# Attention in twelve batches of 2 to 4 chunks for fourteen of 3, with squares on VectorE, other opening matmuls and the last copy on ScalarE

## The chip, the core and the metric

The program runs on one core of one Trainium2 chip. The core has TensorE (PE in the rows, with PEld for its weight loads), VectorE (DVE), ScalarE (ACT), GpSimd (POOL) and SyncE (SP), which issues most of the transfers. Each engine takes its own instructions in program order and waits for the others through semaphores. The metric is the time of one execution on the device in microseconds (us).

## The reference

Sigmoid attention over 2 batches, 12 heads, 448 positions and 64 dimensions, then two MLPs on the 896 tokens of width 768. All in float32.

```python
def _attn_ref(q, k, v):                 # (2, 12, 448, 64) each
    scale = 1.0 / np.sqrt(q.shape[-1])
    scores = scale * np.matmul(q, k.transpose(0, 1, 3, 2)) - np.log(S)
    attn = 1.0 / (1.0 + np.exp(-scores))
    return np.matmul(attn, v)

def _moe_ref(x, w_gate, w_val, w_out, rms_g):     # 768 -> 1536 -> 768
    rms = np.sqrt(np.mean(x * x, axis=-1, keepdims=True) + 1e-06)
    xn = x / rms * rms_g
    g = xn @ w_gate
    return (g * (1.0 / (1.0 + np.exp(-g))) * (xn @ w_val) @ w_out)

def _moe2_ref(x, w_in, w_out):                    # 768 -> 2048 -> 768
    h = x @ w_in
    return (h * (1.0 / (1.0 + np.exp(-h))) @ w_out)
```

## The kernel before

**Attention.** Two heads are worked on together, as a pair: there are twelve pairs, six to a batch of the input. The 448 keys of a pair are cut into three chunks of 128 (c = 0 to 2) and a tail of 64 keys; the tails of two neighbouring pairs make one chunk together (c = 3, called with the even pair). That gives 42 chunks. `scores(i, c)` makes the scores of one chunk of pair i: three passes of matmuls, each for two heads (high times high, low times high, high times low parts of keys and queries), or one float32 pass for a tail and for the first chunk of pairs 0 and 1. They go into a tile of the pool `scp`, which has three, each two banks wide; then ScalarE applies the sigmoid (L387) and writes a tile of the pool `at`. `attend(i, c)` multiplies such a tile by the values (L405) into the accumulator of the pair, one bank of the pool `avp`, which has two. When a pair has its four contributions, `collect(i)` copies the accumulator to `xr` (VectorE, L420 or L425) and squares it (ScalarE, L423), and `add_square` adds the square to the batch's sum (VectorE, L431). `prep(i)` splits keys and queries of a pair into high and low parts (VectorE).

**Turns.** The loop at L530 runs over batches of `BATCH` = 3 chunks. In each turn it collects what is ready, issues the scores of the turn's batch (tail last), adds the squares, and then issues the attends of the batch before (tail first). Behind that come the letters of the turn's entry in `PLAN`: each `w` is the next step of `prologue`, each `n` the next step of `norm_first`. Nothing reorders these instructions (`manual_schedule`): the program's order is each engine's order.

`prologue` has 26 steps. They prepare six slabs of weights and cut the first four of them into high and low parts: for a slab s there is the exponent (ScalarE, L253), the shift (VectorE, L257), the merge (VectorE, L265) together with the load of the slab two ahead on SyncE's queue, the cast of two halves (ScalarE, L241) and their lower parts (VectorE, L244). In the order of the steps the cast of slab s-1 stands behind the exponent of slab s, and its lower parts behind the shift of slab s.

`norm_first` normalises the first batch of the input. Its steps: square sums (`square_sums`, eight one-column matmuls, L436); the first half of `rsqrt` (six small VectorE operations); the second half (six more, then `diag`, L456, 448 wide); an empty step; the spread of `diag` over all partitions (a matmul, L473) with ScalarE's copy `r` of it (L499); then eight steps of `normed`, in each of which one block of `xr` is scaled (L481), the one before it gets its high part (ScalarE, L241) and the one before that its low part (VectorE, L244).

**After attention.** The two MLPs follow. All their work is made of jobs for which `Plan.run` sets the order by costs and due times. It begins with a product of the normalised first batch (`g`, L730); behind that product the square sums of the second batch (L436) stand in TensorE's queue, one product later their spread (L473). The last block of the output is made in `mixed` (L831 on): the accumulator `e2x` is copied to `e2s` and sent out by SyncE.

**Opening.** While the first loads are under way TensorE runs `IDLE` = 8 matmuls on a tile of zeros (L515), into the tile `idle` of the pool `scp`.

Of the kernel before, what the change touches and what calls it, by code (L numbers as in the profile page):

```python
# [9 lines left out]
F32 = mybir.dt.float32  # L10
F32R = mybir.dt.float32r
BF16 = mybir.dt.bfloat16
U32 = mybir.dt.uint32
I32 = mybir.dt.int32
AF = mybir.ActivationFunctionType
ALU = mybir.AluOpType
PSUM = bass.MemoryType.PSUM

B, H, S, D = 2, 12, 448, 64
# [3 lines left out]
P = 128  # L23
CP = 112
NC = S // CP
KC = S // P
# [3 lines left out]
HALF = 3 * P  # L30
NT = B * S
EPS = 1e-6
BATCH = 3
DIRECT = ((0, 0), (1, 0))
IDLE = 8
SQUARED = 10
LAG = {"A": 0.105, "D": 0.081, "P": 0.165, "S": 4.4}
HOP = 0.4
# [5 lines left out]
ZI = True  # L44
ZE = False
LOADED = (6, 7)
PLAN = ",,ww,w,www,www,ww,ww,wwn,wwnn,wwnn,wwwnn,wwnn,wwnn,nn".split(",")
LOADS = (0, 2)
RING = 9
RESERVE = 6  # L50
# [143 lines left out]
def tile_attention_two_mlps(  # L194
# [9 lines left out]
    nc = tc.nc  # L204
# [8 lines left out]
    sp = ctx.enter_context(tc.tile_pool(name="sp", bufs=1))  # L213
# [103 lines left out]
    xr = [rp.tile([P, 2, 2, S], F32, tag=f"r{t}", name=f"xr{t}") for t in range(3)]  # L317
    ctx.enter_context(tc.manual_schedule())
    with ExitStack() as actx:
        ap = actx.enter_context(tc.tile_pool(name="ap", bufs=2))  # L320
        at = actx.enter_context(tc.tile_pool(name="at", bufs=8))
        pctx = ExitStack()
        psum = [pctx.enter_context(tc.tile_pool(name="scp", bufs=3, space=PSUM))]
        avp = pctx.enter_context(tc.tile_pool(name="avp", bufs=2, space=PSUM))
# [2 lines left out]
        kq, vr, ks, att, av, acc, sqs = {}, {}, {}, {}, {}, {}, {}  # L327
# [4 lines left out]
        def load_pair(i):  # L332
            b, hp = pairs[i]
            if i not in kq:
                pair_tile(i)
            if i:
                nc.sync.dma_start(kq[i], kqd[b, hp])
            else:
                for j, queue in enumerate((nc.sync, nc.scalar)):
                    queue.dma_start(kq[i][:, j], kqd[b, hp, :, j])  # L340
# [49 lines left out]
        begun = {}  # L390
# [24 lines left out]
        def collect(i):  # L415

            b, hp = pairs[i]
            ps = av.pop(i)[:, :S]
            if i < SQUARED:
                nc.vector.tensor_copy(xr[hp // 2][:, b, hp % 2], ps)  # L420
            which, home_ = ("s1", sqs) if hp else ("s0", acc)
            sq = home_[i if hp else b] = sp.tile([P, S], F32, tag=which, name=f"{which}{i}")
            nc.scalar.activation(sq, ps, AF.Square)  # L423
            if i >= SQUARED:
                nc.vector.tensor_copy(xr[hp // 2][:, b, hp % 2], ps)  # L425

        def add_square(i):

            b, hp = pairs[i]
            if hp:  # L430
                nc.vector.tensor_tensor(acc[b], acc[b], sqs.pop(i), ALU.add)  # L431
# [71 lines left out]
        n = len(pairs)  # L503
        normal = norm_first()
        load_pair(0)
        zeros = sp.tile([P, S], F32, tag="s3", name="zeros").bitcast(BF16)[:, :P]
        nc.vector.memset(zeros, 0.0)
        nc.vector.memset(warm, 0.0)
        nc.vector.memset(logs, -6.104793232414985)
        nc.vector.memset(ones, 1.0)  # L510
        nc.scalar.activation(warm, warm, AF.Sigmoid)
        row = zeros[:, None, :D].to_broadcast([P, S // D, D])
        idle = ps_tile("idle")
        for j in range(IDLE):
            nc.tensor.matmul(idle[:, j % 2, :S], zeros, row, start=True, stop=True)  # L515
        load_pair(1)
        pair_tile(2)
        nc.vector.memset(kq[2], 0.0)
# [7 lines left out]
        turn_, ready = 0, []  # L526
        chunks = []
        for i in range(0, n, 2):
            chunks += [(i, c) for c in range(KC + 1)] + [(i + 1, c) for c in range(KC)]
        batches = [chunks[j : j + BATCH] for j in range(0, len(chunks), BATCH)]  # L530
        for before, batch in zip([[]] + batches, batches + [[]]):
            for i in ready:
                collect(i)
            for i, c in sorted(batch, key=lambda u: u[1] == KC):
                if c == 0:
                    if i + 1 < n:
                        prep(i + 1)
                    if i + 3 < n:
                        load_pair(i + 3)
                        load_v(i + 3)  # L540
                    if i in LOADS:
                        load_next()
                scores(i, c)
            while ready:
                add_square(ready.pop(0))
            for i, c in sorted(before, key=lambda u: u[1] != KC):
                ready += attend(i, c)
            for what in PLAN[turn_]:
                if what == "w":
                    step()  # L550
                else:
                    next(normal, None)
            turn_ += 1
        collect(ready[0])
        add_square(ready.pop())


        for _ in normal:
# [15 lines left out]
    def dve(n, fn, deps=(), **more):  # L574
        return plan.add("D", 0.071 + n / 960, fn, deps, **more)
# [224 lines left out]
    sdone = [None] * 4  # L800
# [52 lines left out]
    def mixed(  # L853
        name, macs, slabs, keys, book, fdep, put, dest=None, home=None, ahead=True, own=None, finish=None, per=6
    ):


        n = len(keys)
        w = [6 * (slabs + i // per) + i % per for i in range(2 * n)]
        saved = {}  # L860

        def save(j, src, dep):
            def go():
                saved[j] = saved_tile(name, j)
                nc.scalar.activation(saved[j], src(), AF.Copy)

            return scalar(S, go, [dep, sdone[j]], psum=True)

        def add(j, src, deps, m=None, b=None):
            def go():  # L870
                d = saved[j] if m is None or dest is None else dest(m, b)
                tt(d, src(), saved[j], ALU.add)

            a = dve(S, go, deps, need=home.ready if dest and m is not None else None)
            if m is not None:
                sdone[j] = put(m, b, lambda: saved[j] if dest is None else dest(m, b), a) or a
            return a

        g = lambda ps, a, **k: group(macs, ps, a, book, fdep, own, **k)
        if ahead:  # L880
            bx, by = Banks(f"{name}x"), Banks(f"{name}y")
            ba, bb = Banks(f"{name}a", True), Banks(f"{name}b", True)
            bz, bv, bu, bw = ba.bank(0), ba.bank(1), bb.bank(0), bb.bank(1)
            done = []
            for k in range(0, n, 2):
                for m, t in enumerate((ba, bb)):
                    i = 2 * k + 2 * m
                    done += product(
                        [t.bank(0), t.bank(1)], w[i : i + 2], keys[k : k + 2], (0, 1), first=k == 0,
                        final=k == n - 2 and m > 0, take="ps" if k == 0 else None, start=t.start if k == 0 else None,  # L890
                    )
            u = save(3, bu, done[-1])
        else:
            bx, by, bz, bw = (Banks(f"{name}{c}") for c in "xyzw")
        g1 = g(bx, "A11", start=True, first=bx)
        v0 = save(0, bx, g1)
        g2_ = g(by, "S1", start=True, first=by)
        v1 = save(1, by, g2_)
        g3 = g(bx, "S2", deps=[v0])
        v2 = save(2, bx, g3)  # L900
        g4 = g(bz, "A12", start=not ahead, stop=ahead, first=None if ahead else bz)
        if ahead:
            a00 = add(0, bz, [g4, v0], 0, 0)
        g5 = g(bx, "S3", deps=[v2])
        a11 = add(1, bx, [g5, v1])
        if ahead:
            c11 = add(1, bw, [a11], 1, 1)
            bb.read_by(u, c11)
        g6 = g(by, "S4", stop=ahead, deps=[v1])
        if ahead:  # L910
            a01 = add(2, by, [g6, v2])
            c01 = add(2, bv, [a01], 0, 1)
            by.read_by(v1, a01)
            ba.read_by(a00, c01)
        g7 = g(bx, "A22", stop=ahead, deps=[a11])
        if ahead:
            a10 = add(3, bx, [g7, u], 1, 0)
            bx.read_by(a10)
            return
        p0 = product([bz, by], w[:n], keys, (0, 1), first=False)  # L920
        a00 = add(0, bz, [p0[-1], v0], 0, 0)
        a01 = add(2, by, [p0[-1], v2], 0, 1)
        bz.read_by(a00)
        by.read_by(v1, a01)
        p1 = product([bx, bw], w[n:], keys, (1,), last=False, take="one", start=bw.start)
        c11 = add(1, bw, [p1[-1], a11], 1, 1)
        bw.read_by(c11)
        p2 = product([bx, bw], w[n:], keys, (0,), first=False)

        if finish:  # L930
            bx.read_by(finish(bx, p2[-1]))
            return

        def copy():
            saved[3] = saved_tile(name, 3) if dest is None else dest(1, 0)
            nc.vector.tensor_copy(saved[3], bx())

        a10 = dve(S, copy, [p2[-1], sdone[3]])
        bx.read_by(a10)
        sdone[3] = put(1, 0, lambda: saved[3], a10)  # L940

# [190 lines left out]
    for k in ORDER:  # L1132
# [5 lines left out]
        n_ = dve(1.13 * S, scale, [r_])  # L1138
# [98 lines left out]
    for t in range(3):  # L1237
        dest = lambda m, b, t=t: r2[t]()[:, b, m]
        n = 0 if t < 2 else 3
# [66 lines left out]
    for p in range(3):  # L1306
        wide_ = 1 if p == 0 else 2
        keys = [("g", k) for k in range(6 + 2 * wide_, K2)]
        n = 0 if p < 2 else 4
# [101 lines left out]
```

## Time and profile before

| | us |
|---|---|
| median of three runs | 528.5 |
| lowest, highest of them | 528.39, 1331.32 |
| the profiled execution | 530.01 |
| its span (first to last instruction) | 528.2 |
| TensorE busy in the span | 522.7 |
| VectorE busy | 444.9 |
| ScalarE busy | 364.9 |

The span is what the views of the trace divide up; the profiled execution's own time lies 1.8 us above it.

### The profile page before, as it was taken

Reading aid. Unit: us, or ns where it says so; the run is one execution under the profiler, and the core shown is the slowest. Engines: PE = TensorE matmul, PEld = TensorE weight load, DVE = VectorE, ACT = ScalarE, POOL = GpSimd, SP = SyncE. Lnnn points to the kernel's source line nnn. Section 1 sums busy time; section 2 is a strip of 40 time slices with the busy share of each in tenths; the row PEclk is TensorE's granted clock in tenths of the full one; section 3 lists DMA queues with packets and bytes.
Section 4 is the critical chain, followed back from the end, with each engine's and each line's share of the span. In section 5 each row is a group of like instructions: output and inputs, shape, how many; then the busy total and the mean of one; then the engine's idle time right before and its main releaser. Section 6 shows DMA issues by size and latency. Waiting matters only on the chain.

```text
span 528.2 us, 7375 instructions
## 1 busy us (share of the span) xinstructions
PE 522.7 (99%) x2691; PEld 449.6 (85%) x2691; DVE 444.9 (84%) x825; ACT 364.9 (69%) x638; POOL 0.2 (0%) x4
## 2 busy tenths in 40 slices
PE   9999999999999999999999999999999999999997
PEld 4445469999999999999999999999889999999996
DVE  6579789999998988799989989998776999988601
ACT  5887864787888686867596788998766947363500
POOL 0000000000000000000000000000000000000000
PEclk9999999999999999999999999999999999999999
DMA  8744321031524343411633442433343230627001
GB/s 319 267 180 166 107 72 60 1 120 61 181 72 167 122 179 95 147 42 53 204 101 119 158 163 78 153 106 141 130 151 120 99 120 29 221 83 247 20 1 70
DMA packets 16292, 65.01 MB, mean 123 GB/s; under 512 B 2048, under 2 KB 4608, under 8 KB 16256
## 3 DMA queue, kind: packets, MB, share of 16 engines
q1 hardware_dynamic: 16112, 64.32, 35.5%
q8 instruction: 21, 0.34, 0.3%
q10 hardware_dynamic: 144, 0.23, 0.1%
q14 instruction: 15, 0.12, 0.1%
HBM read 61.79 MB, written 2.75 MB: 122 GB/s over the span
## 4 chain that ended last, share of the span: by engine, by line
PE 86%; DVE 8%; DMA 3%; issue 1%; ACT 1%; DVEq 0%; ACTq 0%
PE av L405 7%; PE sc L378 6%; DMA raw<-in_w 3%; PE g L730 3%; PE v L730 3%; PE e2x L779 2%; PE e1x L779 2%; DVE f L265 2%; PE e0b L730 2%; PE e0a L730 2%; PE e0x L779 2%; PE o2x L779 2%; PE o1x L779 2%; PE o0x L779 2%; PE i7x L779 1%; PE i6x L779 1%
## 5 line engine op out<-in xcount | busy, mean ns | idle before, releaser
L265 DVE SCALAR_TENSOR_TENSOR f<-f,raw 128x768 uint32<-128x768 uint32 (+1 forms) x67 | 60.8, 909 | 8.2 <-ACT f L253 6.7
L253 ACT ACTIVATE f<-raw 128x768 f32<-128x768 f32 (+1 forms) x67 | 57.9, 866 | 6.3 <-DMA raw<-in_w 2.3
L241 ACT ACTIVATE w_S<-f 128x384 fp32r<-128x384 f32 (+1 forms) x78 | 39.3, 506 | 26.2 <-DVE f L688 9.6
L244 DVE TENSOR_TENSOR w_S<-f,w_S 128x384 fp32r<-128x384 f32 (+1 forms) x78 | 41.7, 536 | 9.5 <-ACT w_S L241 9.0
L261 ACT ACTIVATE raw<-raw 128x768 int32<-128x768 uint32 (+1 forms) x50 | 42.4, 849 | 9.7 <-DMA raw<-in_w 9.5
L387 ACT ACTIVATE a<-sc,logs 128x896 f32<-128x896 f32 x42 | 39.1, 1011 | 6.4 <-PE sc L378 6.4
L241 ACT ACTIVATE w_A<-f 128x384 fp32r<-128x384 f32 (+1 forms) x75 | 36.9, 507 | 7.3 <-DVE f L265 3.0
L244 DVE TENSOR_TENSOR w_A<-f,w_A 128x384 fp32r<-128x384 f32 (+1 forms) x75 | 39.5, 540 | 1.1 <-ACT w_A L241 0.9
L405 PE MATMUL av<-a,vr 128*64 128x448 f32 (+1 forms) x192 | 35.5, 552 | 0.0
L405 PEld LDWEIGHTS av<-a,vr 128*64 128x64 f32 (+1 forms) x192 | 10.5, 135 | 21.3 <-issue 20.1
L378 PEld LDWEIGHTS sc<-ks 64*128 64x128 f32 x204 | 18.6, 189 | 10.1 <-ACT f L253 2.8
L378 PE MATMUL sc<-ks 64*128 64x448 f32 x204 | 25.3, 385 | 0.0
L244 DVE TENSOR_TENSOR w<-f,w 128x384 fp32r<-128x384 f32 (+1 forms) x36 | 17.2, 493 | 6.4 <-ACT w L241 6.4
L241 ACT ACTIVATE w<-f 128x384 fp32r<-128x384 f32 (+1 forms) x36 | 16.4, 476 | 8.2 <-PE e2x L779 2.1
L241 ACT ACTIVATE w_S<-s 128x384 fp32r<-128x384 f32 x23 | 12.0, 521 | 4.8 <-PE g L730 3.1
L730 PE MATMUL g<-x,w 128*128 128x448 f32 x72 | 15.3, 368 | 0.0
L730 PE MATMUL v<-x,w 128*128 128x448 f32 x72 | 15.3, 370 | 0.0
L257 DVE TENSOR_SCALAR raw<-raw 128x768 uint32<-128x768 uint32 (+1 forms) x24 | 12.5, 523 | 2.9 <-DMA raw<-in_w 2.9
L730 PEld LDWEIGHTS g<-x,w 128*128 128x128 f32 x72 | 13.4, 188 | 1.8 <-issue 0.7
L730 PEld LDWEIGHTS v<-x,w 128*128 128x128 f32 x72 | 13.5, 188 | 1.4 <-issue 0.4
L695 DVE TENSOR_TENSOR f<-f 128x384 f32<-128x384 f32 (+1 forms) x26 | 13.9, 535 | 0.1
L420 DVE COPY xr<-av 128x448 f32<-128x448 f32 x10 | 6.2, 624 | 9.1 <-PE av L405 9.1
(1402 smaller groups left out, 1475.5 us busy)
## 6 DMA issues: line engine op xcount, KB each, us to landing
raw<-in_w SPq DMA_DIRECT2D x56, 768.0 KB, 4.4
raw<-in_w SPq DMA_DIRECT2D x18, 512.0 KB, 3.5
kq<-in_kq SPq DMA_DIRECT2D x11, 448.0 KB, 5.4
vr<-in_v SPq DMA_DIRECT2D x6, 256.0 KB, 5.0
vr<-in_v SPq DMA_DIRECT2D x6, 192.0 KB, 3.7
out_t<-e0s SPq DMA_DIRECT2D x4, 224.0 KB, 4.3
out_t<-e1s SPq DMA_DIRECT2D x4, 224.0 KB, 2.3
out_t<-e2s SPq DMA_DIRECT2D x4, 224.0 KB, 1.9
```

Source lines behind the costliest of these rows:

```text
L241: nc.scalar.activation(dst, src, AF.Copy)
L244: nc.vector.tensor_tensor(dst, src, hi.bitcast(F32), ALU.subtract)
L253: nc.scalar.activation(floats[s], words(s)[:, :, 1].bitcast(F32), AF.Prelu, scale=2.0**-112, alpha=2.0**32)
L257: nc.vector.tensor_scalar(z, z, 29, None, ALU.logical_shift_right)
L261: nc.scalar.activation(z.bitcast(I32), z, AF.Copy, scale=2.0**-29 * (1 - 2.0**-18), bias=-0.5 + 2.9e-5)
L265: nc.vector.scalar_tensor_tensor(fu, fu, 3, words(s)[:, :, 0], ALU.logical_shift_left, ALU.bitwise_or)
L378: nc.tensor.matmul(ps[to, h, :S], k_[:, keys], q_, start=(step == 0), stop=(step == 2 or plain), skip_group_check=True,)
L387: nc.scalar.activation(a, ps[:, :, :S], AF.Sigmoid, bias=logs, scale=D**-0.5)
L405: nc.tensor.matmul(av[n][h * D : (h + 1) * D, :S], vr[i][rows, c, h, :], a[rows, h, :], start=(begun[n] == 1), stop=(begun[n] == KC + 1), ...
L695: s4 = dve(hw, lambda: tt(block(1), block(1), block(0), ALU.subtract), [s2, l3])
L730: nc.tensor.matmul(banks[b](), t[:, jw], act[key](jx, b), start=(first and i == 0 and n_ == 0), stop=(final and i == n - 1 and n_ == 2), s ...
L779: nc.tensor.matmul(ps(), w[:, jw, j * P : (j + 1) * P], book[t][USES[a]][jx], start=(start and i == 0 and n == 0), stop=(stop and i == len ...
```

## The change

The batches get the sizes of a list, 2 to 4 chunks in twelve batches instead of 3 in fourteen. `PLAN` has thirteen entries for fifteen and other letters in them. The pool `at` has 11 tiles for 8. At the head of a turn, all ready pairs but the last are collected and their squares added one after the other; between attends a ready pair may be collected as well, where a new pair would find no bank. The attends of a turn are sorted by the couple of pairs first. For the first ten pairs the square is a VectorE multiplication of the copied block with itself, behind the copy. The opening has nine matmuls, on a constant one that the program's start has set already, and no tile of zeros. The copy of the last block of the output is a ScalarE pass; where `mixed` has another destination it stays on VectorE.

```diff
--- before.py
+++ after.py
@@ -30,9 +30,9 @@
 HALF = 3 * P
 NT = B * S
 EPS = 1e-6
-BATCH = 3
+SIZES = [2, 4, 4, 4, 3, 4, 3, 4, 3, 4, 4, 3]
 DIRECT = ((0, 0), (1, 0))
-IDLE = 8
+IDLE = 9
 SQUARED = 10
 LAG = {"A": 0.105, "D": 0.081, "P": 0.165, "S": 4.4}
 HOP = 0.4
@@ -44,7 +44,7 @@
 ZI = True
 ZE = False
 LOADED = (6, 7)
-PLAN = ",,ww,w,www,www,ww,ww,wwn,wwnn,wwnn,wwwnn,wwnn,wwnn,nn".split(",")
+PLAN = ",,w,wwwww,wwwww,,wwwww,wwnnnnn,wwn,wnw,nwww,nnnwn,nnn".split(",")
 LOADS = (0, 2)
 RING = 9
 RESERVE = 6
@@ -318,7 +318,7 @@
     ctx.enter_context(tc.manual_schedule())
     with ExitStack() as actx:
         ap = actx.enter_context(tc.tile_pool(name="ap", bufs=2))
-        at = actx.enter_context(tc.tile_pool(name="at", bufs=8))
+        at = actx.enter_context(tc.tile_pool(name="at", bufs=11))
         pctx = ExitStack()
         psum = [pctx.enter_context(tc.tile_pool(name="scp", bufs=3, space=PSUM))]
         avp = pctx.enter_context(tc.tile_pool(name="avp", bufs=2, space=PSUM))
@@ -416,13 +416,15 @@
 
             b, hp = pairs[i]
             ps = av.pop(i)[:, :S]
-            if i < SQUARED:
-                nc.vector.tensor_copy(xr[hp // 2][:, b, hp % 2], ps)
             which, home_ = ("s1", sqs) if hp else ("s0", acc)
             sq = home_[i if hp else b] = sp.tile([P, S], F32, tag=which, name=f"{which}{i}")
-            nc.scalar.activation(sq, ps, AF.Square)
-            if i >= SQUARED:
-                nc.vector.tensor_copy(xr[hp // 2][:, b, hp % 2], ps)
+            xi = xr[hp // 2][:, b, hp % 2]
+            if i < SQUARED:
+                nc.vector.tensor_copy(xi, ps)
+                nc.vector.tensor_tensor(sq, xi, xi, ALU.mult)
+            else:
+                nc.scalar.activation(sq, ps, AF.Square)
+                nc.vector.tensor_copy(xi, ps)
 
         def add_square(i):
 
@@ -503,16 +505,14 @@
         n = len(pairs)
         normal = norm_first()
         load_pair(0)
-        zeros = sp.tile([P, S], F32, tag="s3", name="zeros").bitcast(BF16)[:, :P]
-        nc.vector.memset(zeros, 0.0)
         nc.vector.memset(warm, 0.0)
         nc.vector.memset(logs, -6.104793232414985)
         nc.vector.memset(ones, 1.0)
         nc.scalar.activation(warm, warm, AF.Sigmoid)
-        row = zeros[:, None, :D].to_broadcast([P, S // D, D])
+        square, row = (nc.const_aps.tensor(1.0, [P, n_], BF16) for n_ in (P, S))
         idle = ps_tile("idle")
         for j in range(IDLE):
-            nc.tensor.matmul(idle[:, j % 2, :S], zeros, row, start=True, stop=True)
+            nc.tensor.matmul(idle[:, j % 2, :S], square, row, start=True, stop=True)
         load_pair(1)
         pair_tile(2)
         nc.vector.memset(kq[2], 0.0)
@@ -527,8 +527,11 @@
         chunks = []
         for i in range(0, n, 2):
             chunks += [(i, c) for c in range(KC + 1)] + [(i + 1, c) for c in range(KC)]
-        batches = [chunks[j : j + BATCH] for j in range(0, len(chunks), BATCH)]
+        batches = [[chunks.pop(0) for _ in range(n)] for n in SIZES]
         for before, batch in zip([[]] + batches, batches + [[]]):
+            while len(ready) > 1:
+                collect(ready[0])
+                add_square(ready.pop(0))
             for i in ready:
                 collect(i)
             for i, c in sorted(batch, key=lambda u: u[1] == KC):
@@ -543,7 +546,10 @@
                 scores(i, c)
             while ready:
                 add_square(ready.pop(0))
-            for i, c in sorted(before, key=lambda u: u[1] != KC):
+            for i, c in sorted(before, key=lambda u: (max(0, u[0] // 2 - before[0][0] // 2), u[1] != KC)):
+                if ready and len(av) > 1 and any(n_ not in begun for n_ in ((i, i + 1) if c == KC else (i,))):
+                    collect(ready[0])
+                    add_square(ready.pop(0))
                 ready += attend(i, c)
             for what in PLAN[turn_]:
                 if what == "w":
@@ -551,8 +557,9 @@
                 else:
                     next(normal, None)
             turn_ += 1
-        collect(ready[0])
-        add_square(ready.pop())
+        for i in ready:
+            collect(i)
+            add_square(i)
 
 
         for _ in normal:
@@ -933,9 +940,9 @@
 
         def copy():
             saved[3] = saved_tile(name, 3) if dest is None else dest(1, 0)
-            nc.vector.tensor_copy(saved[3], bx())
-
-        a10 = dve(S, copy, [p2[-1], sdone[3]])
+            (nc.vector.tensor_copy if dest else high)(saved[3], bx())
+
+        a10 = (dve if dest else scalar)(S, copy, [p2[-1], sdone[3]])
         bx.read_by(a10)
         sdone[3] = put(1, 0, lambda: saved[3], a10)
 
```

## Rows read from the trace of the kernel before

**Rows 1.** Part 1 of the page: each engine's busy time, share of the span, instructions.

```profile
PE 522.7 (99%) x2691; PEld 449.6 (85%) x2691; DVE 444.9 (84%) x825; ACT 364.9 (69%) x638; POOL 0.2 (0%) x4
```

**Rows 2.** Waits of TensorE, whole span: waiter, releaser, us in total, times, longest.

```profile
PE idle L515 <- DVE logs L509: 1.0, 1, 1.0
PE i5x L779 <- DVE g L817: 0.3, 1, 0.3
```

**Rows 3.** Chain that ended last, 0 to 100: start us, us, engine, tile, line.

```profile
9.83 2.41 PE av L405 x12
12.24 2.02 PE sc L378 x18
14.26 2.57 PE av L405 x16
16.83 2.33 PE sc L378 x20
...
44.63 0.88 PE ms L436 x8
...
54.84 0.95 PE r L473 x2
...
72.06 3.84 PE g L730 x18
```

**Rows 4.** Timeline, weight loads of attends: start us, us, engine, line, operation, count, idle before.

```profile
10.57 0.14 PEld L405 LDWEIGHTS av<-a,vr 128*64 128x64 f32 x2 [0.23 <-issue]
...
10.94 0.14 PEld L405 LDWEIGHTS av<-a,vr 128*64 128x64 f32 x2 [0.23 <-issue]
```

**Rows 5.** Timeline of the second normalisation (TensorE and VectorE).

```profile
76.46 3.96 PE L730 MATMUL g<-x,w 128*128 128x448 f32 x18
76.64 0.16 DVE L444 TENSOR_SCALAR rsqrt<-v 112x4 f32<-112x4 f32 x1 [0.99 <-PE v L436]
...
79.02 0.62 DVE L456 TENSOR_TENSOR diag<-spare,rsqrt 112x448 f32<-112x448 f32 x1
```

**Rows 6.** Groups of VectorE, then ScalarE, 0 to 72: busy us, mean ns, idle.

```profile
L265 DVE SCALAR_TENSOR_TENSOR f<-f,raw 128x768 uint32<-128x768 uint32 x6 | 5.7, 953 | 0.0
L431 DVE TENSOR_TENSOR s<-s,s 128x448 f32<-128x448 f32 x9 | 5.6, 620 | 3.8 <-ACT s L423 3.8
...
L423 ACT ACTIVATE s<-av 128x448 f32<-128x448 f32 x11 | 6.0, 546 | 4.0 <-DVE xr L420 3.9
```

**Rows 7.** Timeline of VectorE at the start of one turn.

```profile
40.07 0.62 DVE L420 COPY xr<-av 128x448 f32<-128x448 f32 x1
...
40.60 0.62 DVE L354 CAST ks<-kq 128x896 fp32r<-128x896 f32 x1
...
42.27 0.62 DVE L431 TENSOR_TENSOR s<-s,s 128x448 f32<-128x448 f32 x1
```

**Rows 8.** Timeline of ScalarE: the three sigmoids of one turn.

```profile
13.08 2.80 ACT L387 ACTIVATE a<-sc,logs 128x896 f32<-128x896 f32 x3 [1.59 <-PE sc L378]
```

**Rows 9.** Timeline, ScalarE before the second normalisation's copy; the page's part 6, slab loads.

```profile
81.21 0.55 ACT L1128 ACTIVATE r<-v 128x448 f32<-128x448 f32 x1 [5.19 <-PE v L473]
...
raw<-in_w SPq DMA_DIRECT2D x56, 768.0 KB, 4.4
```

**Rows 10.** Timeline of the opening.

```profile
0.81 0.11 DVE L507 MEMSET zeros<- 128x64 uint32 x1 [0.81 <-PEq L1401]
...
1.70 0.15 PEld L515 LDWEIGHTS <-zeros 128*128 128x128 bf16 x1 [0.22 <-issue]
...
2.08 0.15 PEld L515 LDWEIGHTS <-zeros 128*128 128x128 bf16 x1 [0.22 <-issue]
...
4.08 1.87 PE L378 MATMUL sc<-kq 64*128 64x448 f32 x4
...
7.29 0.91 PE L378 MATMUL sc<-kq 64*128 64x448 f32 x4
```

**Rows 11.** Timeline of the end.

```profile
524.32 0.62 DVE L936 COPY e2s<-e2x 128x448 f32<-128x448 f32 x1 [3.02 <-PE e2x L730]
```

## The prediction

> **What bounds the kernel now.** Read the page's first part first: TensorE (PE) is busy for 522.7 us of the span of 528.2 us [rows 1]. Busy can hide waiting, so the waits come next: TensorE's longest is the 1.0 us before its first matmul, and no other reaches 0.4 us [rows 2]. Then the chain that ended last: from 0.98 us on it is a gapless list of TensorE pieces, through attention (to 72.06 us) and the two MLPs [rows 3]. So inside this kernel VectorE (DVE) and ScalarE (ACT) cost nothing unless TensorE has to wait for them, and each us that TensorE is made to work less, or to wait, shows in the end time.
>
> Since nothing is waited for, the chain prices each piece. An attend chunk takes two steps of 0.375 us [rows 4], 0.75; three chunks take 2.41, so leaving the attend form costs about 0.15. A tail attend with two chunks takes 2.57, which makes the tail 0.92 with its own change of form. Three scored chunks take 2.02; two and a tail take 2.33; with the same 0.92 for that tail a scored chunk is 0.61 and the change behind the scores 0.19 [rows 3].
>
> **The new order of the queues.** The letters of PLAN and the loop give each engine's order; the kernel keeps program order there (in the trace of before the square sums at 44.63 and the spread at 54.84 stand where the letters put them [rows 3]). I list turns T0 to T12 by their TensorE work, all with the prices above, from the first attend at 9.83; what TensorE does ahead of it is the same list as before.
> T1: two attends, 1.65. T2: four scores, tail, three attends, 2.63 + 3.32 = 5.95. T3: three scores with tail, four attends, 2.94 + 3.16 = 6.10. T4, T6, T8: three scores, tail, three attends, 2.02 + 3.32 = 5.34 each. T5, T7, T9: three scores with tail, three attends, 2.94 + 2.41 = 5.35 each. T10: three scores and both tails side by side, 2.02 + 0.75 + 3.32 = 6.09. T11: 5.19 (nothing is scored behind it). T12: three attends, 2.41. Add the square sums, 0.88, and the spread, 0.95 [rows 3]. Sum 61.3; before it is 72.06 - 9.83 = 62.2, so 0.9 less. Counted the other way, two turns less save four changes of form (2 x 0.19 + 2 x 0.15 = 0.68) and the joined tails another 0.17. I take this, since the change from attends to the full-width matmuls behind them is not in my list: **gain 0.85 us.**
>
> **A wait that is put in.** PLAN's eighth entry is `wwnnnnn`. Five `n` run norm_first from its start through the square sums, both halves of rsqrt, the empty yield, and the spread. On TensorE the spread (L473) then stands directly behind the square sums (L436), and behind both stand all scores of T8. But the spread reads diag, which VectorE makes from the square sums: twelve small operations, each on the one before it, and the 448-wide diag. Before, two turns of scores and attends lay between (44.63 and 54.84). The price stands in the second normalisation, where VectorE was idle and waiting: TensorE went on at 76.46, VectorE began at 76.64, and diag began at 79.02 and took 0.62, to 79.64 [rows 5]. So 3.18 us from the end of the square sums; with the way back to TensorE (the same order as the 0.18, I take 0.07 as the weights can be loaded ahead) **loss 3.25 us**, between 3.0 and 3.5. VectorE is not late for it: ahead of rsqrt it has collects of pairs 4 and 5 with their squares and sums (6 x 0.53), a prep (1.67, two rows' start to start), and two slab steps (1.9), 6.8 us, of which the first collect, its square and its sum (1.6) don't wait for T6's last attend; the other 5.2 do, and T7's TensorE work up to the end of the square sums is 5.35 + 0.88 = 6.2. ScalarE's copy of the spread (r) is behind it and T8's first sigmoid behind that; 0.55 us, over before T8's first score ends.
>
> **Squares on VectorE.** Ten ScalarE squares of 546 ns go, ten VectorE multiplies like the adds of 620 ns come [rows 6]. ScalarE gets 5.5 us back and nobody waits for it: 0. The accumulator bank is now free after VectorE's copy alone, not after ScalarE's square too. Each attend that opens a bank comes at least 2 us after its collect in my list, but for T11, whose tail opens two at once and needs the copy of pair 9, due about 1 us earlier: 0, at worst 0.4. VectorE's last stretch is the tight one. From T8 on (l3, the lower parts of slab 3, waits for ScalarE's cast behind T8's sigmoids; T8 begins near 50.1, so near 54.3) it holds 27 operations of 448 columns (6 scalings, 6 lower parts, 6 copies, 4 squares, 5 sums), two preps and five slab steps. At start to start, 0.53 for one [rows 7], that is 14.3 + 3.3 + at most 4.8 = 22.4 us, to 76.7; at their busy times (0.62) 24.9, to 79.2. A slab step is at most 953 ns [rows 6]. What waits at the end is the square sums of batch 1, one product (3.84 us [rows 3]) behind attention's end: with that end at 74.6 (below) they are wanted at 78.5. So 0 by the spacing and 0.7 by the busy times; I take 0, as rows 7 show the spacing in a full queue.
>
> **Four scores, three score tiles.** In T2 the fourth score takes the tile of the first, whose sigmoid starts 0.9 us after the score and takes 0.93 (the turn whose scores begin at 12.24 has its three sigmoids from 13.08 on, 2.80 in all [rows 3, 8]): 2.63 - 0.61 = 2.02 is when the fourth would start and 0.9 + 0.93 + about 0.2 when it may: 0.1 us of wait; bounds 0 and 0.5. In the other turns of four the last is a tail, 0.2 later: 0.
>
> **Weight steps moved.** Their 26 letters are the same; the slab loads they issue on SyncE's queue go with them. By the list slabs 1 and 2 come 0.5 to 1 us later, and slab 7, sent for by the last merge, some 2 us nearer to attention's end (behind T11's collects of two pairs instead of one). The first to miss slab 7 is ScalarE, and what covers it is ScalarE's idle time, 5.19 us ahead of the second normalisation's copy; without that cover up to the load's landing, 4.4 us, would show [rows 9]. 0. The 11 attention tiles for 8 take no time.
>
> **Opening and end.** The first matmul no longer waits for VectorE's memset of zeros: it can start when the engines do, near 0.8 [rows 10]. The ninth adds 0.37 (from 1.70 to 2.08 [rows 10]); 0.8 + 9 x 0.373 = 4.15 against the first score at 4.08: **loss 0.06**. Last copy: 0.62 on VectorE [rows 11] against 0.55 for a ScalarE pass from such a bank [rows 6]: **gain 0.07**.
>
> **Sum.** -0.85 + 3.25 + 0.1 + 0.06 - 0.07 = +2.5; attention ends at 72.06 + 2.55, about 74.6. The profiled execution took 530.01 us for its span of 528.2, the median is 528.5; the difference carries over: **531.0 us**.
>
> **TensorE's clock.** The opening shows the lower level: 448 columns per 0.373 us are 1.2 GHz, 0.375 for the two passes of an attend step are 2.4. The same four records take 1.87 at 4.08 and 0.91 at 7.29 [rows 4, 10], and the pieces of the chain behind keep the faster pace [rows 3]. Rival: the stall, with 0.88 us of one-column matmuls ahead of it, lets the clock fall, and T8 starts at 1.2 GHz. It would then take up to what the opening took, from 0.98 to at most 7.29, to rise: 6.3 us at half speed, up to 3.1 lost, about 2 likely: 532 to 534. For it: 4.1 us almost without work is more than any stretch of before after 1 us. Against: it is short. The Trainium skill, in TensorE: Matmul & The Clock Gate (What's actually happening), says that the half rate is the default, that activity releases it and that an idle engine falls back; the opening rows agree with the first part, no row here shows the second.
>
> **Other rivals.** (1) Faster: the wait is not there, since diag is ready when the spread comes up. It decides at a wait under 0.85. Then 528.5 - 0.85 + 0.1 = 527.7, and 526.8 if the earlier opening also raises the clock before the first score (1.87 - 0.91 = 0.96). For it: the trace of before has no such wait. Against: there two turns lay between, here none. (2) VectorE, with 6.2 us more to do, is late at attention's end as well: by busy times 0.7, with a late copy of pair 9 another 0.4, 531.4 to 532.1. (3) The change does not do what it says: fewer turns save nothing, since the changes of form are paid anyway; then 531.8, inside the range.
>
> **Numbers.** Forecast with the wait, 530.3 to 531.8: 0.62. Clock falls: 0.15. VectorE late: 0.13. No wait: 0.10. The range takes the first and third, half of the clock's, and the earlier rise of the clock beside the wait (530.0): 529.5 to 533.2. Faster or slower by over 2% (10.6 us, about what a measurement can tell from no change) is beyond every case here: 0.01 and 0.02 for what I did not see.
>
> **What would show it.** Right: a TensorE wait of the spread for VectorE's diag of about 3.2 us near 46 to 49; attention's end, the first g matmul, at 74 to 75; attend-to-score pieces as priced; ten L431-like squares on VectorE; the last copy on ScalarE at 0.55. Wrong: the spread right behind the square sums with no wait; T8's scores at twice their 2.02 (clock); waits of scores for sigmoids; the square sums of batch 1 late.

## The result and the profile after

The changed kernel takes 532.94 us (median of five; 532.17 to 535.24) where the kernel before takes 528.44 in the same comparison. The ratio is 1.0091, 95% interval 1.0064 to 1.0117: slower by 0.9%, 3.4 to 6.2 us. 531.0 us was forecast; 528.5 x 1.0091 = 533.3 lies just above the range (533.2).

First the waits of TensorE, whole span (waiter, releaser, us in total, times, longest). The first line is new against [rows 2]; it is the wait that the prediction put behind the square sums, 3.2 us.

```profile
PE r L475 <- DVE diag L458: 3.2, 1, 3.2
PE idle L515 <- PEq L1408: 0.8, 1, 0.8
PE i5x L786 <- DVE g L824: 0.3, 1, 0.3
PE sc L378 <- DMA kq<-in_kq: 0.2, 1, 0.2
```

Then the chain that ended last, 0 to 110 us (start us, us, engine, tile, line), to be laid beside [rows 3].

```profile
9.10 1.65 PE av L405 x8
10.75 2.79 PE sc L378 x24
13.54 3.32 PE av L405 x20
16.86 2.94 PE sc L378 x26
...
41.91 2.40 PE av L405 x12
44.31 0.89 PE ms L438 x8
...
47.60 0.64 DVE diag L458
...
48.37 1.83 PE r L475 x2
50.21 3.66 PE sc L378 x15
53.86 3.80 PE av L405 x20
57.66 2.96 PE sc L378 x26
...
76.73 3.84 PE g L737 x18
80.57 0.69 PE v L438 x8
```

Up to the square sums (ms) every turn has the length that the list gave within 0.03 us, but for T2, whose four scores take 2.79 for 2.63: the fourth's weight load stands 0.27 us for ScalarE's first sigmoid of the turn, the wait for the score tile. From the first attend, 9.10, to ms, 44.31, it is 35.21 us; the list has 1.65 + 5.95 + 6.10 + 5.34 + 5.35 + 5.34 + 5.35 = 35.08, and 0.1 for the score tile. Then 44.31 + 0.89 = 45.20 to 48.37 is the standstill, 3.17. Behind it the spread takes 1.83 where it took 0.95 [rows 3], the three scored chunks 3.66 for 2.02, the attends 3.80 for 3.32. From 57.66 on all has its old price. The windows of that stretch say what it was (window, its length; busy us and count of PE, PEld, DVE, ACT and POOL; granted clock; DMA share; GB/s).

```profile
40.00:46.00 6.00, 5.19 (x38) 2.42 (x36) 4.94 (x11) 3.52 (x4) 0.00 (x0) 1.00 0.53 196
46.00:50.00 4.00, 1.63 (x2) 0.50 (x2) 3.55 (x11) 0.00 (x0) 0.00 (x0) 0.75 0.68 273
50.00:52.00 2.00, 2.00 (x11) 1.69 (x12) 0.00 (x0) 0.81 (x2) 0.00 (x0) 0.50 0.00 0
52.00:54.00 2.00, 2.00 (x14) 1.32 (x16) 0.00 (x0) 1.83 (x3) 0.00 (x0) 0.50 0.02 4
54.00:56.00 2.00, 2.00 (x14) 0.45 (x12) 0.64 (x2) 1.74 (x3) 0.00 (x0) 0.80 0.03 8
56.00:60.00 4.00, 4.00 (x32) 2.24 (x32) 3.90 (x8) 1.49 (x2) 0.00 (x0) 1.00 0.14 49
```

The granted clock fell to 0.50, TensorE's 1.2 GHz, during the standstill and came back between 54 and 56 us. The three longer pieces hold 0.88 + 1.64 + 0.48 = 3.0 us that it cost.

A measure that leaves the opening out is used from here on: **W**, from the first attend to the square sums of batch 1. In the chain of the kernel before, from which [rows 3] are taken, those stand at:

```profile
75.91 0.69 PE v L436 x8
```

So W is 75.91 - 9.83 = 66.08 before and 80.57 - 9.10 = 71.47 after. The difference, 5.39, is 3.17 + 3.0 - 0.85 + 0.1 = 5.42. The first attend itself came 0.73 earlier (9.10 for 9.83), because the clock rose earlier in this execution: the first score's four records take 1.02 us for 1.87 [rows 10].

```profile
4.19 1.02 PE L378 MATMUL sc<-kq 64*128 64x448 f32 x4 [0.17 <-DMA kq<-in_kq]
```

5.4 - 0.7 = 4.7, the step of attention's end (76.73 for 72.06). The medians' step, 4.5, agrees, since the profiled execution of after is also the median one. The other four are made up in another way. Each execution's mean granted clock is recorded: 0.992 in the profiled one, 0.995 to 0.997 in the others. So the 3.0 us are the most of the five; in the traces of e3 and e4 below, with 0.995 and 0.997, the fall costs 1.5 and 1.6.

The two profiled executions lie only 2.9 apart (532.94 and 530.01). The step is still 4.6 at 315 us; the other 1.7 are lost by 440 us. Of these 0.8 lie ahead of the tile i6y (391 us in the trace of before). The other 0.9 lie from its first piece to the first of e0y, with no wait of TensorE between: 46.50 us before and 45.61 after, at a granted clock of 1.00 in both. What slows the trace of before there it doesn't show. It is not the kernel: the piece of that stretch from e0a to e0x takes 19.84 us in four of the fourteen traces (before, e2, e3 and e8 below) and 19.45 or 19.46 in the other ten.

The small edits read as forecast. Groups of VectorE and ScalarE (columns as in [rows 6]): the ten squares are multiplications of 625 ns, and the last copy takes 0.54 us for 0.62 [rows 11] (no run tells what that gives in time).

```profile
L424 DVE TENSOR_TENSOR s<-xr 128x448 f32<-128x448 f32 x10 | 6.3, 625 | 0.3
...
L241 ACT ACTIVATE e2s<-e2x 128x448 f32<-128x448 f32 x1 | 0.5, 543 | 21.4 <-PE e2x L737 21.4
```

### The profile page after: what moved, and what is told of

It is laid out like the page before. It is cut to its first block, busy times and chain, and to the rows that moved or that the text cites. A ratio compares the mean times of both kernels' runs of the same rounds, so it can differ in the third digit from the quotient of the medians.

```text
span 531.1 us, 7381 instructions
## 1 busy us (share of the span) xinstructions
PE 522.8 (98%) x2692; PEld 450.6 (85%) x2692; DVE 450.5 (85%) x833; ACT 361.4 (68%) x629; POOL 0.2 (0%) x4
## 4 chain that ended last, share of the span: by engine, by line
PE 85%; DVE 8%; DMA 4%; issue 1%; ACT 1%; DVEq 0%; ACTq 0%
PE av L405 6%; PE sc L378 6%; DMA raw<-in_w 3%; PE g L737 3%; PE v L737 3%; PE e1x L786 2%; PE e2x L786 2%; DVE f L265 2%; PE e0a L737 2%; PE o1x L786 2%; PE o0x L786 2%; PE e0x L786 2%; PE e0b L737 2%; PE o2x L786 2%; PE i7x L786 1%; PE g5x L786 1%
## 5 line engine op out<-in xcount | busy, mean ns | idle before, releaser
L265 DVE SCALAR_TENSOR_TENSOR f<-f,raw 128x768 uint32<-128x768 uint32 (+1 forms) x67 | 60.8, 909 | 8.3 <-ACT f L253 6.7
```

What stands on the lines that cost most here:

```text
L265: nc.vector.scalar_tensor_tensor(fu, fu, 3, words(s)[:, :, 0], ALU.logical_shift_left, ALU.bitwise_or)
```

## The experiments

All of these ran later than the result above, with runs of the kernel before beside them that have medians of 529.0 to 529.3 us and go from 527.4 to 531.3. Times are therefore read as ratios to the runs beside them, and mechanisms in the traces by W. (Some expectations give W by the timeline, 0.1 to 0.2 us lower than by the chain, as here.)

| run | W, us | median, us | ratio to before, 95% |
|---|---|---|---|
| before | 66.08 | 529.0 to 529.3 | 1 |
| after | 71.47 | 532.94 (before: 528.44) | 1.0091 (1.0064 to 1.0117) |
| e1_spread_n | 66.88 | 529.92 | 1.0017 (1.0000 to 1.0033) |
| e2_fill | 68.55 | 531.52 | 1.0058 (1.0037 to 1.0080) |
| e3_before_five | 70.86 | 533.74 | 1.0100 (1.0075 to 1.0126) |
| e4_old_opening | 70.14 | 534.55 | 1.0103 (1.0067 to 1.0140) |
| e5_rsqrt_first | 65.94 | 528.80 | 0.9994 (0.9978 to 1.0010) |
| e6_spread_sq_act | 74.66 | 537.82 | 1.0156 (1.0128 to 1.0184) |
| e7_rsqrt_first_sq_act | 69.85 | 532.50 | 1.0064 (1.0043 to 1.0085) |
| e8_before_new_opening | 66.09 | 529.16 | 0.9996 (0.9980 to 1.0011) |
| e9_merge_last | 65.94 | 528.73 | 1.0000 (0.9985 to 1.0015) |
| e10_fill8 | 70.05 | 531.57 | 1.0051 (1.0026 to 1.0076) |
| e11_before_sq_dve | 66.71 | 531.88 (one run) | |
| e12_merge_behind | 65.29 | 528.54 | 0.9992 (0.9981 to 1.0003) |

### Is it the wait, and is the clock's fall its consequence?

**e2_fill** keeps the wait and gives TensorE something to do in it.

```diff
+            fill = ps_tile("fill")
+            for j in range(16):
+                nc.tensor.matmul(fill[:, j % 2, :S], square, row, start=True, stop=True)
             diag = yield from rsqrt(0, ps[:, 0])
```

> The changed kernel with sixteen matmuls of 448 columns on the constant one between the square sums and the spread (3.0 us of work that nothing reads). My theory: the wait for diag stays, but the clock does not fall, so 3.0 us come back: 529.9 (529.4 to 530.4), with the granted clock 1.00 through 46 to 56 us. Rival, the fall of the clock is not from the standstill: 532.9 as before, clock 0.5 there. Rival, the loss behind the stall is something else than the clock: 532 to 533 with clock 1.00.

The chain of this run, 0 to 90 us:

```profile
44.55 0.88 PE ms L438 x8
45.42 3.09 PE fill L497 x16
48.60 0.99 PE r L475 x2
49.59 2.05 PE sc L378 x18
51.64 3.32 PE av L405 x20
```

The spread starts 3.17 us behind the square sums, as it did; but behind it 0.99, 2.05 and 3.32 are the full clock's prices, and the granted clock is 1.00 in every window from 40 to 60 us, of which one (columns as above):

```profile
50.00:52.00 2.00, 2.00 (x20) 1.36 (x22) 0.12 (x1) 1.67 (x3) 0.00 (x0) 1.00 0.06 12
```

W falls from 71.47 to 68.55, by 2.9 of the 3.0 us. So the fall comes from TensorE having nothing to do, and what is left over the kernel before, 2.5 us, is the wait less the turns. The expected time came out 1.6 too low: it was worked out from the earlier medians and from the 3.0 us of one execution. By the ratios of the medians (1.0091 and 1.0058) the filling gives back 1.7 us. The ratio, 1.0058, is 3.1 us (2.0 to 4.2) and holds the 2.5.

**e10_fill8** has eight of the sixteen matmuls, so that half the standstill stays.

```diff
-            for j in range(16):
+            for j in range(8):
```

> The kernel of e2_fill with eight of its sixteen matmuls: 1.5 us of work behind the square sums, then about 1.7 us of standstill. Theory: the whole standstill is what the clock fell for, half of it is harmless: granted clock 1.00 through, attention ends as in e2 and the time is that of e2 (531.5) within the spread. Rival: the shorter standstill also lets the clock fall: 0.5 somewhere in 46 to 58 us and 1.5 to 3 us more.

Waits, then windows of the run:

```profile
PE r L475 <- DVE diag L458: 1.6, 1, 1.6
```

```profile
48.00:50.00 2.00, 0.74 (x2) 0.30 (x2) 1.86 (x6) 0.00 (x0) 0.00 (x0) 1.00 0.82 334
50.00:52.00 2.00, 2.00 (x11) 1.65 (x12) 0.78 (x1) 0.95 (x2) 0.00 (x0) 0.60 0.02 9
52.00:54.00 2.00, 2.00 (x14) 1.26 (x15) 0.00 (x0) 1.84 (x3) 0.00 (x0) 0.55 0.05 12
```

In this execution the rival was right: the standstill was 1.6 us, the clock fell just behind it, and W is 1.5 above e2's. The medians of the two (531.57 and 531.52) don't tell them apart, and the mean granted clocks of the executions say why: 0.997 in this one, the slowest of the five, and 0.999 to 1.000 in the other four, where the theory held. In the kernels that keep 3.2 us of standstill (after and, below, e3 and e4) all thirteen executions have 0.992 to 0.997; in those without a standstill of over 1.5 us, e2 with them, every one has 0.998 to 1.000. So with half the standstill the clock fell in one execution of five, with the whole in all.

**e3_before_five** does nothing of the change but put five steps into one turn of the old kernel.

```diff
-PLAN = ",,ww,w,www,www,ww,ww,wwn,wwnn,wwnn,wwwnn,wwnn,wwnn,nn".split(",")
+PLAN = ",,ww,w,www,www,ww,ww,wwnnnnn,ww,ww,wwwnn,wwnn,wwnn,nn".split(",")
```

> The kernel before with only one thing of the change: five steps of norm_first in one turn (the ninth entry wwnnnnn, the two behind it without n). Batches of three, squares, opening and last copy as before. My theory: wait of 3.2 us and up to 3.0 for the clock: 534.6 (533.5 to 535). Rival, the fall hung on where the turn happened to stand: 528.44 + 3.2 = 531.6. Rival, the wait needs the new batches: 528.4.

The waits of TensorE, and the chain behind the square sums:

```profile
PE r L473 <- DVE diag L456: 3.2, 1, 3.2
```

```profile
44.47 0.89 PE ms L436 x8
...
48.52 0.99 PE r L473 x2
49.51 3.38 PE sc L378 x18
52.89 2.73 PE av L405 x16
```

Same wait, and a fall again: 3.38 for 2.02 and 2.73 for 2.57, 1.5 us here. W grows by 4.8, 3.2 + 1.5. The letters alone make the old kernel slower, by as much as the whole change. The cost of the clock is not fixed: 3.0 us in the trace of after, 1.5 here and 1.6 in e4.

**e4_old_opening** is the changed kernel with the zeros, the old wait and eight matmuls.

```diff
-IDLE = 9
+IDLE = 8
...
+        zeros = sp.tile([P, S], F32, tag="s3", name="zeros").bitcast(BF16)[:, :P]
+        nc.vector.memset(zeros, 0.0)
...
-        square, row = (nc.const_aps.tensor(1.0, [P, n_], BF16) for n_ in (P, S))
+        row = zeros[:, None, :D].to_broadcast([P, S // D, D])
```

> The changed kernel with the opening of before: eight matmuls on a zeroed tile, behind VectorE's memset. My theory: the clock rises later again, the first score takes 1.87 for 1.02 us, and 0.7 us are lost: 533.6 (533.3 to 534). Rival, the earlier rise was this execution's luck: 532.9, and the first score at either pace in the trace.

Its runs go from 531.59 to 535.24 and the interval holds the changed kernel's ratio: it decides nothing on the opening by itself. **e8_before_new_opening**, the inverse edit in the kernel before, tells more.

> The kernel before with the opening of the change alone (nine matmuls on the constant one). Theory: the clock rises earlier, within 3.4 to 4.6 us as in the three traces with this opening (4.9 to 6.5 in the three with the old one), the first attend is at 8.8 to 9.3 instead of 9.3 to 9.8, and the time falls by 0.4 to 0.9 us. Rival: the rise comes at any time in any execution whatever the opening; the median is then that of the kernel before within 0.3 us.

The ratio is 0.9996 (0.9980 to 1.0011): no difference, within 1.1 us to the faster side and 0.6 to the slower. The first attend came at 9.36. Over all traces it lies at 9.83, 9.64, 9.39 and 9.83 with the old opening and at 9.10, 8.88, 9.32, 9.57, 9.22, 9.21, 9.36, 9.97, 9.97 and 9.71 with the new one. When the clock rises differs from execution to execution by more than the two openings do, if they do: the means, 9.67 and 9.43, are 0.24 apart. The 0.73 us of the trace of after are for the most part that execution's, not the change's.

### What are the batches worth without the wait?

**e1_spread_n** takes the wait away by letters alone: the same steps over three turns.

```diff
-PLAN = ",,w,wwwww,wwwww,,wwwww,wwnnnnn,wwn,wnw,nwww,nnnwn,nnn".split(",")
+PLAN = ",,w,wwwww,wwwww,,wwwww,wwn,wwnn,wnwn,nnwww,nnnwn,nnn".split(",")
```

> The changed kernel with the same letters in PLAN, but the steps of norm_first over three turns (one in the eighth entry, two in the ninth, two in the tenth, spread there), so that scores and attends lie between the square sums and the spread. My theory (the 4.5 us are the wait for diag, 3.2, plus 3.0 from the lower clock behind it, less 0.85 for the turns and 0.7 for the opening): wait and clock loss both gone, 528.44 - 0.85 - 0.7 + 0.1 = 527.0, within 526.4 to 527.8. Rival, the batches themselves cost time (scores waiting for tiles, VectorE late at attention's end): 529 to 530. Rival, the clock falls for another reason: 530.

The wait for diag is gone and the clock stays, but W is 66.88, 0.8 above the kernel before instead of 0.85 below it: the first rival. The chain of this run goes over VectorE from 49.33 us on. Timeline of VectorE:

```profile
49.33 1.03 DVE L244 TENSOR_TENSOR w<-f,w 128x384 fp32r<-128x384 f32 x2 [3.56 <-ACT w L241]
50.28 0.15 DVE L446 TENSOR_SCALAR rsqrt<-ms 112x4 f32<-112x4 f32 x1
```

It stood for 3.56 us at the lower part of a slab, which waits for ScalarE's cast behind three sigmoids, with 3 us of rsqrt, ready to run, queued behind that instruction. In the changed kernel VectorE did its rsqrt while TensorE stood, and was ahead.

**e5_rsqrt_first** turns the letters of that turn round.

```diff
-PLAN = ",,w,wwwww,wwwww,,wwwww,wwn,wwnn,wnwn,nnwww,nnnwn,nnn".split(",")
+PLAN = ",,w,wwwww,wwwww,,wwwww,wwn,nnww,wnwn,nnwww,nnnwn,nnn".split(",")
```

> The kernel of e1_spread_n with one entry of PLAN turned round: in the turn behind the square sums both halves of rsqrt stand ahead of the two weight steps (nnww for wwnn). In e1 VectorE stood idle for 3.56 us there, waiting for ScalarE's cast, with rsqrt (3.0 us) queued behind the waiting instruction, and was the chain from there to attention's end. Theory: that was the loss; rsqrt now lies in the idle time, VectorE ends 3 us earlier, TensorE is the chain again, and the second product (g) ends its first block with no wait: 1.5 to 2 us less than e1 from first attend to the square sums of batch 1 (66.7 us in e1, 66.0 in the kernel before; 65.0 here). Rival: ten squares on VectorE are too much in any order; then VectorE is still the chain and it stays at 66 or above.

VectorE's wait there shrinks to 0.45 us and W to 65.94, 0.9 less than e1, not the 1.5 to 2 expected: the first product after attention still waited for lower parts of x.

**e9_merge_last** moves the last merge behind the normalisation's steps.

```diff
-PLAN = ",,w,wwwww,wwwww,,wwwww,wwn,nnww,wnwn,nnwww,nnnwn,nnn".split(",")
+PLAN = ",,w,wwwww,wwwww,,wwwww,wwn,nnww,wnwn,nnwww,nnnnnnw,n".split(",")
```

> The kernel of e5_rsqrt_first with the last merge (and the slab load that it sends for) moved behind the six last steps of the normalisation, all in the turn before the last. In e5 the first product after attention still waited for lower parts of x that stood behind that merge and behind the collect of pair 10 in VectorE's queue. Theory: TensorE is the chain throughout, the batches are worth what the sum said: 65.1 us from first attend to the square sums of batch 1 (65.9 in e5, 66.1 in the kernel before), and 0.6 to 1.2 us under the kernel before on the same chip. Rival: the later slab load or ScalarE's high parts take its place; then 65.7 or more.

Attention now takes what the sum said, 61.4 us from first attend to first product (62.2 before), but W stays at 65.94, as the rival had it, though by another way. The waits of TensorE, then the timeline:

```profile
PE v L438 <- DVE s L433: 0.7, 1, 0.7
```

```profile
71.90 0.95 DVE L265 SCALAR_TENSOR_TENSOR f<-f,raw 128x768 uint32<-128x768 uint32 x1
72.77 0.61 DVE L427 COPY xr<-av 128x448 f32<-128x448 f32 x1
73.31 0.61 DVE L433 TENSOR_TENSOR s<-s,s 128x448 f32<-128x448 f32 x1
74.03 0.55 ACT L426 ACTIVATE s<-av 128x448 f32<-128x448 f32 x1 [2.61 <-DVE s L433]
```

The merge (L265) stands ahead of the sum of pair 10 (L433). ScalarE's square of pair 11 waits for that sum, as there is one tile for squares, and the last sum waits for the square.

**e12_merge_behind** puts the merge behind that sum.

```diff
-PLAN = ",,w,wwwww,wwwww,,wwwww,wwn,nnww,wnwn,nnwww,nnnnnnw,n".split(",")
+PLAN = ",,w,wwwww,wwwww,,wwwww,wwn,nnww,wnwn,nnwww,nnnnnn,nw".split(",")
```

> The kernel of e9_merge_last with the last merge one step further back, behind the collect and the sum of pair 10. In e9 attention took 61.4 us from first attend to the first product, as the sum of the turns said, but the square sums of batch 1 then waited 0.7 us: VectorE's merge stood ahead of the sum of pair 10, ScalarE's square of pair 11 waited for that sum, and the last sum for the square. Theory: the whole chain comes 0.9 us earlier and the wait goes: 65.2 to 65.4 us from first attend to the square sums of batch 1 (65.9 in e9, 66.1 in the kernel before), 0.4 to 1 us under the kernel before on the same chip. Rival: the last sum is late all the same, since the square of pair 11 is; 65.7 or more, and no measurable difference.

Waits of TensorE, whole span, and the chain at the first attend and at attention's end:

```profile
PE idle L515 <- PEq L1408: 0.8, 1, 0.8
PE i5x L786 <- DVE g L824: 0.7, 1, 0.7
```

```profile
9.71 1.65 PE av L405 x8
...
71.16 3.85 PE g L737 x18
75.00 0.77 PE v L438 x8
```

Every wait of attention is gone, and W is 75.00 - 9.71 = 65.29, 0.79 under the kernel before: the gain that the sum gave the twelve batches. In time it is 0.9992 (0.9981 to 1.0003): not to be told from the kernel before (nor from e5 and e9), but by the two ratios some 5 us better than the change as it was made. By W it is the best version found.

### What the squares on VectorE are for

**e6_spread_sq_act** (on e1) and **e7_rsqrt_first_sq_act** (on e5) put the squares back on ScalarE.

```diff
-                nc.vector.tensor_tensor(sq, xi, xi, ALU.mult)
+                nc.scalar.activation(sq, ps, AF.Square)
```

> The kernel of e1_spread_n with the ten squares back on ScalarE (read from the accumulator bank, as before); all else stays. If VectorE's extra 6.2 us made e1 no faster than the kernel before, then from first attend to the square sums of batch 1 it takes 65.0 to 65.5 us (66.7 in e1). Rival: ScalarE, with sigmoids of a turn and the squares, now holds the scores back, and it takes 66 or more with waits of scores for sigmoids.

> Both: rsqrt ahead of the weight steps and the ten squares on ScalarE. If TensorE alone is the chain then, the batches are worth the 0.85 us of the sum: 65.0 us from first attend to the square sums of batch 1, and a time 1 us under the kernel before on the same chip. If the squares on VectorE have a use (a bank freed earlier), this is slower than e5_rsqrt_first by 0.3 or more.

Both are slower, W 74.66 for 66.88 and 69.85 for 65.94 (in e6, whose longest wait of a score is 2.7 us, the clock fell as well: 0.997 on the mean in all three executions). In both the theory missed and the alternative named with it held. Of e7's 3.9 us over e5, 2.7 stand in three waits of scores for sigmoids, and 0.9 in a longer wait of the first product behind attention (1.3 for 0.4). The timeline of e7 in a turn that collects two pairs:

```profile
28.82 0.62 DVE L433 TENSOR_TENSOR s<-s,s 128x448 f32<-128x448 f32 x1 [1.72 <-ACT s L424]
29.36 0.62 DVE L423 COPY xr<-av 128x448 f32<-128x448 f32 x1
...
30.07 0.54 ACT L424 ACTIVATE s<-av 128x448 f32<-128x448 f32 x1 [1.28 <-DVE xr L423]
30.51 3.70 ACT L387 ACTIVATE a<-sc,logs 128x896 f32<-128x896 f32 x4
...
31.57 0.98 PE L378 MATMUL sc<-kq 64*64 64x448 f32 x8 [1.15 <-ACT a L387]
```

The turn collects pairs 2 and 3. ScalarE's second square waits 1.28 us for VectorE's copy, behind the sum that frees the square tile; the turn's four sigmoids are queued behind that square, and TensorE's tail score waits 1.15 us for a score tile. With both square and copy on VectorE nothing of this crosses engines.

**e11_before_sq_dve** moves only the squares in the kernel before: in `collect` the same lines as in the change.

> The kernel before with only the ten squares on VectorE. With batches of three, two pairs are never collected in one turn, so no sigmoid stands behind a second square; the squares' place should be worth nothing: 66.1 us from first attend to the square sums of batch 1 as in the kernel before, at most 0.8 more if VectorE ends late. Rival: the squares on ScalarE cost in the old batches too, then 65.5 or less.

W is 66.71, 0.6 more, within what was expected; 0.5 of it is one wait of a score for VectorE's rsqrt, which is late. In batches of three the move costs a little, in the one execution there is. So the squares on VectorE belong to the new batches and are of no use alone.

## Why the prediction was right and where it was wrong

**The price list and the order of the queues** held: every turn within 0.1 us, the wait at 3.17 for 3.25, the gain of the turns less the score tile at 0.79 (e12) for 0.85 - 0.1, the last copy at 0.54 for 0.55. The score tile's 0.1 doesn't come out of its own working (2.02 against 0.9 + 0.93 + 0.2 leaves 0.01); the scores of that turn took 0.16 longer than listed, by a wait that the trace does show. Reading the letters of PLAN as positions in TensorE's queue gave place and size of the largest term.

**TensorE's clock** is the step that failed. It was left out of the sum, as a rival at 0.15, on the ground that the standstill is short, with about 2 us as its price. It fell in every execution that keeps the 3.2 us of standstill, and cost 3.0 us in the profiled one of after, which the bound of 3.1 held, and 1.5 to 1.6 in those of e3 and e4. So the chance was wrong, and the price about right: with 2 us in the sum the forecast would have been +4.5, as large as the step of the medians. With the profiled execution's own numbers it is 2.5 + 3.0 - 0.06 = +5.4, less the 0.7 by which its clock rose early. The argument "it is short" had no row behind it; the row that was there, the opening at 1.2 GHz [rows 10], showed that an engine that has not worked yet starts at the lower level. The Trainium skill, in TensorE: Matmul & The Clock Gate (What's actually happening), says that an idle engine falls back. The runs now show it: 0.50 behind 3.17 us of standstill in the trace of after, and in one execution of e10 behind 1.6.

**Squares, 0** held in the sum, which has no wait for a square in any turn. Its reason, that nobody waits for ScalarE, was right for the kernel before (e11 gains nothing) and wrong for the new order. The question asked was who waits for ScalarE today; the one to ask was who would wait for the squares where two pairs are collected in one turn. The answer, 3.9 us (e7 against e5), follows from the queue order that the prediction had listed.

**VectorE late, 0 to 0.7 taken as 0** came true in the changed kernel, where VectorE did its rsqrt during the standstill. Without that (e1) VectorE is the chain and costs 1.6 us against e12, whose letters are in another order.

**The opening** was priced at a loss of 0.06 and looked like a gain of 0.73 in the trace of after; e8's interval is too wide to show the first, and the spread of the first attends is wider than the second.

**The chain** was said to be TensorE's alone through both MLPs. [Rows 3] end at 100 us; beyond, from 316 to 387 us, the chain of the kernel before lies on VectorE, ScalarE and three slab loads of 6.0 to 6.3 us. Of attention's step of 4.6 us 3.9 are left behind that stretch; how much of a gain of under 1 us would be, no run shows.

## What to carry to other kernels

When steps are dealt out by a hand-written list, write down the queue of each engine and look for two instructions that stand back to back there and have a chain on another engine between them: that chain's length is the wait, readable from the same chain elsewhere in the trace. Count what TensorE's clock does behind such a wait as part of its price, even for a wait of 2 or 3 us, and give the engine other work there if the wait must stay. An edit that is worth nothing where it is made now can be what another edit needs, so price each in the new order too.

## What the runs showed of the hardware

By the mean granted clock of each execution the clock fell behind a standstill of 3.2 us in thirteen of thirteen, behind one of 2.7 us (e6) in three of three, and behind one of 1.6 us (e10) in one of five. The windows at 0.50 show the lower level in stretches between 48 and 62 us, and its cost was 1.5 to 3.0 us. When it rose in the opening moved the first attend from one execution to the next, between 9.4 and 9.8 us in four traces with the old opening and between 8.9 and 10.0 in ten with the new one. And in four traces of fourteen TensorE took 2% longer for the same matmuls in a stretch near 390 to 440 us, at a granted clock of 1.00, for a reason that no view shows. On one core too, a difference under 2 us has to be read from pieces of the trace rather than from single times.
